# Sparse attention into a MoE layer on one core: rows loaded four to a partition, q/k transposes three tiles earlier, score tiles in front of the MoE units

## The chip, the cores and the metric

One core of a Trainium2 chip runs the kernel. The metric is device time in microseconds (us), lower is better; each median is of several executions on a chip. A "run" below also has one profiled execution, and its profile is what the lines are taken from. All medians are of fast runs alone: runs over 1.5% above the fastest of their kernel are left out. Engines: PE does matmuls, DVE is the vector engine, ACT the scalar engine, POOL is GpSimd, SP issues DMAs and does nothing else in this kernel. In this kernel matmuls write tiles in PSUM and the other tiles lie in SBUF; to "evict" is to copy a result from PSUM to SBUF. The "granted clock" is the share of PE's full clock that the profile records.

## The reference

Per head (8 batches x 8 heads, 576 rows, 64 columns):

```python
scores = scale * q @ k.T
thresh = max(scores, axis=-1) - tau
attn   = softmax(where(scores >= thresh, scores, -1e9))
x      = attn @ v                       # heads put side by side: [4608 tokens, 512]
h = x @ w_in                            # 512 -> 2048
out = leaky_relu(h, 0.01) @ w_out       # 2048 -> 512
```

## The kernel before

Two heads make a pair; a pair has five score tiles (four of 128 queries of both heads, a fifth "half" tile with the 64 last rows of each). A loop step handles two tiles; 160 tiles make 80 steps. MoE work is slipped into the steps: "h units" (first layer; 0.65 us of PE at full clock, 740.58 to 741.23 in the timeline), "o units" (second layer; 3.45 us, 743.36 to 746.81), and PV, the product of weights and v.

```python
def split(P):      # q, k -> high and low fp16 halves: ACT copy, POOL scale, POOL subtract
def turn_qk(P):    # one DMA transpose qk <- nat
def scores(P, i):  # score tile in PSUM, 128 x 1536 fp32, two buffers
def peak(s):       # DVE: mx = row maxima
def exps(s):       # ACT: bi = -mx, e = exp(S + bi)
def weights(s):    # DVE: th = mx - tau; w = (S >= th) * e with its sum; POOL: w *= 1 / sum
def pv(P):         # PE: p1 (512 queries), p2 (64); ACT evicts both into xT, later
# h units, o units and PV share one PSUM tag "m" with two buffers of 128 x 512 fp32

for n in range(0, NT + 10, 2):
    ...
    live.append(scores(tile n)); feed_h(2 or 3); live.append(scores(tile n + 1))
    feed_o()                                  # PV if one is due, else an o unit
    for s in live: peak(s); exps(s)
    for s in live: weights(s)
    flush(evacs)                              # eviction of PV or of the o unit
    for s in turned: turn_w(s)                # DMA transposes of the weights
    ...
    if i == 1: split(P + 2)
    if i == 3: turn_qk(P + 1)
    if i == 3 and P % 2 == 1: load(P + 3), load(P + 4)
```

The kernel issues everything through its class `InOrder`, which keeps the instructions in the order of the program.

## Time and profile before

| | before |
|---|---|
| median (3 runs) | 793.09 us |
| PE / DVE / ACT / POOL busy | 69 / 62 / 50 / 47% |
| mean granted PE clock | 0.836 |
| DVE idle before a row maximum, waiting for scores | 208.1 us |
| PE idle before score matmuls, waiting for the q/k transpose | 134.2 us |

No engine is full, so the waits matter. These lines are from the page's busy times and from the waits view (who waited <- for whom: us in all, times, longest):

```profile
PE 549.5 (69%) x3360; PEld 240.4 (30%) x3360; DVE 487.6 (62%) x1056; ACT 398.6 (50%) x773; POOL 370.0 (47%) x446
DVE mx L31 <- PE S L31: 208.1, 81, 25.2
PE S L31 <- DMA qk<-nat: 134.2, 21, 26.1
PE S L31 <- DVE w L31: 100.9, 48, 5.6
```

DVE waits for PE, and PE mostly for one DMA. Of the 134.2 us, 17.9 are the start of the program and 26.1 one wait while the MoE weights load; the other 19 waits sum to 90.2. In the timeline (start, duration, engine, operation; in brackets the idle time before and what ended it) one such wait looks so:

```profile
200.03 3.45 SPq L31 DMA_TRANSPOSE qk<-nat  x1
205.31 3.72 PE L31 MATMUL S<-qk 64*128 64x512 f16 x18 [6.65 <-DMA qk<-nat]
207.25 1.36 DVE L31 TENSOR_REDUCE mx<-S 128x2 f32<-128x1152 f32 x1 [4.71 <-PE S L31]
212.55 1.09 PE L31 MATMUL S<-qk 64*128 64x512 f16 x9
```

PE was ready at 198.66 (205.31 - 6.65), and the transpose was issued only at 200.03. After the wait, 18 score matmuls take 3.72 us, at a granted clock of 0.50; a few us later, nine take 1.09 at 1.00.

The threshold `th` is two numbers per partition and yet sometimes takes 2 us. The first line below is a tile view (min/median/max ns), the others are the timeline:

```profile
L31 DVE TENSOR_SCALAR th<-mx x160: 132/149/2548, 22.9 to 731.3; 128x2 f32<-128x2 f32 x128, 128x1 f32<-128x1 f32 x32
307.55 2.61 POOL L31 TENSOR_TENSOR nat<-sc,nat 128x1280 f16<-128x1280 f32 x1
308.16 2.03 DVE L31 TENSOR_SCALAR th<-mx 128x2 f32<-128x2 f32 x1
310.28 0.82 DVE L31 SCALAR_TENSOR_TENSOR w<-S,th,e 128x576 f16<-128x576 f32 x1
```

It ends when POOL's subtraction does (307.55 + 2.61 = 310.16). So do the others: each of the 32 thresholds of over 300 ns in this trace ends within 60 ns of the end of a POOL instruction of the split. That is what "blocked by POOL" means below.

### The profile page before, as it was taken

Reading aid. Unit: us, or ns where it says so; the run is one execution under the profiler, and the core shown is the slowest. Engines: PE = TensorE matmul, PEld = TensorE weight load, DVE = VectorE, ACT = ScalarE, POOL = GpSimd, SP = SyncE. Lnnn points to the kernel's source line nnn. Section 1 sums busy time; section 2 is a strip of 40 time slices with the busy share of each in tenths; the row PEclk is TensorE's granted clock in tenths of the full one; section 3 lists DMA queues with packets and bytes.
Section 4 is the critical chain, followed back from the end, with each engine's and each line's share of the span. In section 5 each row is a group of like instructions: output and inputs, shape, how many; then the busy total and the mean of one; then the engine's idle time right before and its main releaser. Section 6 shows DMA issues by size and latency. Waiting matters only on the chain. (4 is left out here: it accounts for less than half of the span.)

```text
span 791.8 us, 10563 instructions
## 1 busy us (share of the span) xinstructions
PE 549.5 (69%) x3360; PEld 240.4 (30%) x3360; DVE 487.6 (62%) x1056; ACT 398.6 (50%) x773; POOL 370.0 (47%) x446
## 2 busy tenths in 40 slices
PE   0440555768666769698775769698785769598998
PEld 0110121323222334234232334233232324243443
DVE  0870777757676667768675667768575667767000
ACT  1440444645454446657454546657454546656333
POOL 6570464454545454555445454555445544623000
PEclk9755675769888789889888789899887789989999
DMA  9689867694869867695769667695859677645201
GB/s 139 128 146 184 172 111 145 102 172 71 167 127 147 130 126 143 121 166 112 160 117 173 118 126 144 113 179 115 160 105 186 105 128 143 118 94 110 64 28 53
DMA packets 377624, 101.90 MB, mean 129 GB/s; under 512 B 370400, under 2 KB 372448, under 8 KB 377568
## 3 DMA queue, kind: packets, MB, share of 16 engines
q1 hardware_dynamic: 337984, 92.31, 61.7%
q0 software_dynamic: 39584, 8.91, 12.2%
q8 instruction: 26, 0.43, 0.2%
q14 instruction: 30, 0.25, 0.1%
HBM read 36.70 MB, written 9.44 MB: 58 GB/s over the span
## 5 line engine op out<-in xcount | busy, mean ns | idle before, releaser
L31 PE MATMUL S<-qk 64*128 64x512 f16 (+2 forms) x1344 | 216.6, 389 | 235.6 <-DMA qk<-nat 134.2
L31 POOL TENSOR_SCALAR w<-w,rc 128x576 f16<-128x576 f16 (+1 forms) x288 | 213.0, 751 | 351.2 <-issue 196.3
L31 DVE TENSOR_REDUCE mx<-S 128x2 f32<-128x1152 f32 (+1 forms) x160 | 198.1, 1242 | 208.6 <-PE S L31 208.1
L31 DVE SCALAR_TENSOR_TENSOR w<-S,th,e 128x576 f16<-128x576 f32 (+1 forms) x288 | 227.4, 823 | 19.6 <-ACT e L31 6.1
L31 ACT ACTIVATE e<-S,bi 128x576 f16<-128x576 f32 (+1 forms) x288 | 200.9, 743 | 5.2
L31 PEld LDWEIGHTS <-qk 64*128 64x128 f16 (+1 forms) x1344 | 74.0, 106 | 391.7 <-DMA qk<-nat 137.3
L31 ACT ACTIVATE gT<-hp 128x384 f16<-128x384 f32 x192 | 94.1, 490 | 186.6 <-PE hp L31 186.4
L31 PE MATMUL op<-w_out_85,gT 128*128 128x512 f16 x576 | 130.3, 380 | 0.0
L31 ACT ACTIVATE bi<-mx 128x2 f32<-128x2 f32 (+1 forms) x160 | 32.1, 201 | 145.6 <-DVE mx L31 145.5
L31 PEld LDWEIGHTS <-w_in_84 128*128 128x128 f16 x768 | 84.1, 112 | 68.6 <-issue 38.6
L31 POOL TENSOR_TENSOR nat<-sc,nat 128x1280 f16<-128x1280 f32 x32 | 83.5, 2609 | 3.9 <-ACT nat L31 1.3
L31 PE MATMUL hp<-xT_86,w_in_84 128*128 128x384 f16 x192 | 73.1, 381 | 2.8 <-ACT xT_88 L31 1.7
L31 PEld LDWEIGHTS <-gT 128*128 128x128 f16 x576 | 55.5, 98 | 61.5 <-issue 1.0
L31 PE MATMUL hp<-xT_87,w_in_84 128*128 128x384 f16 x192 | 72.9, 380 | 0.0
L31 PE MATMUL hp<-xT_88,w_in_84 128*128 128x384 f16 x192 | 72.6, 378 | 0.0
L31 PE MATMUL hp<-xT_89,w_in_84 128*128 128x384 f16 x192 | 71.5, 373 | 0.0
L31 DVE TENSOR_SCALAR th<-mx 128x2 f32<-128x2 f32 (+1 forms) x160 | 53.0, 331 | 0.0
L31 ACT ACTIVATE ob<-op 128x512 f32<-128x512 f32 x36 | 21.5, 597 | 38.1 <-PE op L31 38.1
L31 DVE RECIPROCAL rc<-su 128x2 f32<-128x2 f32 (+1 forms) x160 | 26.4, 165 | 16.9 <-DVE w L31 0.9
L31 PEld LDWEIGHTS <-vt 128*64 128x64 f16 x576 | 24.0, 119 | 21.1 <-issue 8.1
L31 DVE DVE_READ_ACCUMULATOR w<-S,th,e 128x1 f32 x288 | 23.9, 83 | 0.0
L31 ACT ACTIVATE nat<-raw_69 128x1280 f16<-128x1280 f32 x16 | 20.3, 1266 | 6.6 <-DMA raw_69<-in_k_dram 5.9
(186 smaller groups left out, 203.6 us busy)
## 6 DMA issues: line engine op xcount, KB each, us to landing
out_dram<-ob SPq DMA_DIRECT2D x36, 256.0 KB, 2.6
vt<-in_v_dram POOLq DMA_DIRECT2D x8, 576.0 KB, 10.8
raw_69<-in_q_dram SPq DMA_DIRECT2D x32, 128.0 KB, 3.6
raw_69<-in_k_dram SPq DMA_DIRECT2D x32, 128.0 KB, 5.9
raw_70<-in_q_dram SPq DMA_DIRECT2D x32, 128.0 KB, 2.7
raw_70<-in_k_dram SPq DMA_DIRECT2D x32, 128.0 KB, 2.7
W<-w SPq DMA_TRANSPOSE x128, 3.3
w_in_84<-in_moe_w_in_dram POOLq DMA_DIRECT2D x1, 2048.0 KB, 15.6
```

Of the source, the lines that this page charges most:

```text
L31: return self._tc.keep_in_program_order(f(*a, **k))
```

## The change

The intent: larger pieces in the loads, q/k ready in time, second score tile not behind the h units, a threshold that does not meet POOL. Four things change together.

```diff
@@ loads: partition p takes rows 4p .. 4p+3 of a head, 1 KB in one piece; tails of 64 rows apart
-  raws [128, 2, 2, 5, 128]; per pair 128-row blocks of 256 B pieces; vz tiles for the v tails
+  raws [128, 2, 4, 5, 64];  v in vts [128, 8, 5, 64]; no vz
+  main = src[...].rearrange("(h r) d -> h r d", h=n)[:, 0:512, :]
+  dma(out=dst[:, :, 0:4, :]..., in_=main.rearrange("h (p c) d -> p h (c d)", c=4))
@@ split: ACT and POOL copy q and k apart, permuting (h c d) to (c h d)
@@ weights
-  nc.vector.tensor_scalar(out=th, in0=mx, scalar1=-tau_f * UNIT, scalar2=None, op0=ALU.add)
+  nc.vector.scalar_tensor_tensor(out=th, in0=mx, scalar=-tau_f * UNIT, in1=mx, op0=ALU.add, op1=ALU.min)
@@ pv: tile i now holds queries 4t + i, so the eviction puts the tokens back in order
-  nc.scalar.activation(out=xT[g][:, b*S : b*S+512], in_=p1[:, :], func=AF.Copy, ...)
+  nc.scalar.activation(
+      out=xT[g][:, b*S : b*S+512].rearrange("p (t i) -> p i t", i=4),
+      in_=p1[:, :].rearrange("p (i t) -> p i t", i=4), func=AF.Copy, ...)
@@ loop (nh h units are due in a step; tile n's scores were issued at the end of the last step)
-  scores(n); feed_h(nh); scores(n + 1); feed_o(); peak, exps of both; weights of both; flush(evacs)
+  scores(n + 1); peak, exps of both; feed_o(); flush(evacs); feed_h(nh - 1)
+  weights of both; scores(n + 2); feed_h(1)
-  if i == 3: turn_qk(P + 1)
+  if i == 0: turn_qk(P + 1)
```

More of the change, by code (lines that the diff above doesn't have):

```diff
@@ L89 @@
     nc.gpsimd.memset(M2[32:33, 0:64], -60000.0)
-    raws = [sb.tile([128, 2, 2, 5, 128], FP32, name=f"raw_{i}") for i in range(2)]
-    vzs = [sb.tile([128, 2, 64], FP16, name=f"vz_{i}") for i in range(3)]
+    raws = [sb.tile([128, 2, 4, 5, 64], FP32, name=f"raw_{i}") for i in range(2)]
+    vts = [sb.tile([128, 8, 5, 64], FP16, name=f"vt_{i}") for i in range(2)]
     for t in raws:
-        nc.gpsimd.memset(t[0:64, :, :, 4, 64:128], 0.0)
-        nc.gpsimd.memset(t[64:128, :, :, 4, 0:64], 0.0)
-    for t in vzs:
-        nc.gpsimd.memset(t[64:128, 0, :], 0.0)
-        nc.gpsimd.memset(t[0:64, 1, :], 0.0)
+        for h in range(4):
+            nc.gpsimd.memset(t[64 - h % 2 * 64 : 128 - h % 2 * 64, :, h, 4, :], 0.0)
+    for t in vts:
+        for h in range(8):
+            nc.gpsimd.memset(t[64 - h % 2 * 64 : 128 - h % 2 * 64, h, 4, :], 0.0)
     w_in16 = sb.tile([128, NG, d_ff], FP16, name="w_in16")
@@ L104, with heads @@
     pairs = {}
-    vb = {}
+    def heads(dma, dst, src, r0, n):
+        part = src[r0 : r0 + n * S, :].rearrange("(h r) d -> r h d", h=n)
+        main = src[r0 : r0 + n * S, :].rearrange("(h r) d -> h r d", h=n)[:, 0:512, :]
+        dma(out=dst[:, :, 0:4, :].rearrange("p h c d -> p h (c d)"), in_=main.rearrange("h (p c) d -> p h (c d)", c=4))
+        for ab in range(2):
+            dma(out=dst[ab * 64 : ab * 64 + 64, ab::2, 4, :], in_=part[512:576, ab::2, :])
     def load(P):
@@ L110, in load @@
         raw = raws[P // 2 % 2]
+        vt = vts[P // 4 % 2]
         if P % 4 == 0:
-            vb[P // 4] = sb.tile([128, 36, 64], FP16, tag="vt", bufs=2, name="vt")
-            nc.gpsimd.dma_start(
-                out=vb[P // 4][:, :, :], in_=vf[r0 : r0 + 4608, :].rearrange("(c p) d -> p c d", p=128)
-            )
-        for t, (src, oB, tB) in enumerate(((qf, S, S + 512), (kf, S + 64, S))):
-            for ab, o in enumerate((0, oB)):
-                nc.sync.dma_start(
-                    out=raw[:, P % 2, t, 0:4, ab * 64 : ab * 64 + 64],
-                    in_=src[r0 + o : r0 + o + 512, :].rearrange("(c p) d -> p c d", p=128),
-                )
-            if P % 2 == 0:
-                two = src[r0 : r0 + 4 * S, :].rearrange("(u r) d -> r u d", u=2)
-                nc.sync.dma_start(out=raw[0:64, :, t, 4, 0:64], in_=two[512:576])
-                nc.sync.dma_start(out=raw[64:128, :, t, 4, 64:128], in_=two[tB : tB + 64])
-        pairs[P] = dict(raw=raw[:, P % 2], vt=vb[P // 4][:, P % 4 * 9 : P % 4 * 9 + 9, :])
+            heads(nc.gpsimd.dma_start, vt, vf, r0, 8)
+        if P % 2 == 0:
+            for t, src in enumerate((qf, kf)):
+                heads(nc.sync.dma_start, raw[:, t], src, r0, 4)
+        pairs[P] = dict(raw=raw[:, :, P % 2 * 2 : P % 2 * 2 + 2], vt=vt[:, P % 4 * 2 : P % 4 * 2 + 2])
     def split(P):
@@ L131, in split @@
         d["nat"] = nat
-        r2 = d["raw"].rearrange("p t s c -> p t (s c)")
-        sc = sb.tile([128, 2, 640], FP32, tag="sc", bufs=1, name="sc")
-        nc.scalar.activation(out=nat[:, 0, :, :], in_=r2, func=AF.Copy, bias=0.0, scale=PRE)
-        nc.gpsimd.tensor_scalar(out=sc[:, :, :], in0=r2, scalar1=PRE, scalar2=0.0, op0=ALU.mult, op1=ALU.add)
-        nc.gpsimd.tensor_tensor(out=nat[:, 1, :, :], in0=sc[:, :, :], in1=nat[:, 0, :, :], op=ALU.subtract)
+        sc = sb.tile([128, 2, 2, 5, 64], FP32, tag="sc", bufs=1, name="sc")
+        nc.gpsimd.tensor_scalar(
+            out=sc[:, :, :, :, :].rearrange("p t h c d -> p t (h c d)"),
+            in0=d["raw"].rearrange("p t h c d -> p t (h c d)"),
+            scalar1=PRE, scalar2=0.0, op0=ALU.mult, op1=ALU.add,
+        )
+        for t in range(2):
+            o = [nat[:, x, t, :].rearrange("p (c h d) -> p c h d", c=5, h=2) for x in range(2)]
+            nc.scalar.activation(
+                out=o[0], in_=d["raw"][:, t].rearrange("p h c d -> p c h d"), func=AF.Copy, bias=0.0, scale=PRE
+            )
+            nc.gpsimd.tensor_tensor(
+                out=o[1], in0=sc[:, t].rearrange("p h c d -> p c h d"), in1=o[0], op=ALU.subtract
+            )
     def turn_qk(P):
@@ L142, in turn_qk @@
         d["qk"] = qk[:, :, :].rearrange("p a b -> p (a b)")
-    def prep_v(P):
-        d = pairs[P]
-        vz = vzs[P % 3]
-        for ab in range(2):
-            h = slice(ab * 64, ab * 64 + 64)
-            nc.gpsimd.tensor_scalar(
-                out=vz[h, ab, :], in0=d["vt"][h, 4, :], scalar1=1.0, scalar2=0.0, op0=ALU.mult, op1=ALU.add,
-            )
-        d["vz"] = vz
     QH, KH, QL, KL = 0, 640, 1280, 1920
@@ L212, in weights @@
         th = sb.tile([128, 2], FP32, tag="th", bufs=4, name="th")
-        nc.vector.tensor_scalar(out=th[:, 0:n], in0=mx[:, 0:n], scalar1=-tau_f * UNIT, scalar2=None, op0=ALU.add)
+        nc.vector.scalar_tensor_tensor(
+            out=th[:, 0:n], in0=mx[:, 0:n], scalar=-tau_f * UNIT, in1=mx[:, 0:n], op0=ALU.add, op1=ALU.min
+        )
         for h, (po, eo, wd) in enumerate(spans):
@@ L242, in pv @@
         done[0] = P + 1
-        W, Wm, vt, vz = d["W"], d["Wm"], d["vt"], d["vz"]
+        W, Wm, vt = d["W"], d["Wm"], d["vt"]
         b, g = divmod(P, NG)
         p1 = ps.tile([128, 512], FP32, tag="m", bufs=2, name="p1")
-        for n in range(5):
-            for ab in range(2):
-                c = n + 5 * ab if n < 4 else 4
-                lhsT = vt[:, c, :] if n < 4 else vz[:, ab, :]
-                nc.tensor.matmul(
-                    out=p1[ab * 64 : ab * 64 + 64, 0:512], lhsT=lhsT, rhs=W[:, :, c, :],
-                    start=n == 0, stop=n == 4, skip_group_check=True,
-                )
         p2 = ps.tile([128, 512], FP32, tag="m", bufs=2, name="p2")
@@ L258, in pv @@
                 nc.tensor.matmul(
-                    out=p2[ab * 64 : ab * 64 + 64, 0:64], lhsT=vt[:, c, :], rhs=Wm[:, n, ab * 64 : ab * 64 + 64],
+                    out=p1[ab * 64 : ab * 64 + 64, :], lhsT=vt[:, ab, n, :], rhs=W[:, :, c, :],
+                    start=n == 0, stop=n == 4, skip_group_check=True,
+                )
+        for n in range(5):
+            for ab in range(2):
+                nc.tensor.matmul(
+                    out=p2[ab * 64 : ab * 64 + 64, 0:64], lhsT=vt[:, ab, n, :], rhs=Wm[:, n, ab * 64 : ab * 64 + 64],
                     start=n == 0, stop=n == 4, skip_group_check=True,
@@ L263, in evac @@
         def evac():
-            nc.scalar.activation(out=xT[g][:, b * S : b * S + 512], in_=p1[:, :], func=AF.Copy, bias=0.0, scale=1.0)
+            nc.scalar.activation(
+                out=xT[g][:, b * S : b * S + 512].rearrange("p (t i) -> p i t", i=4),
+                in_=p1[:, :].rearrange("p (i t) -> p i t", i=4), func=AF.Copy, bias=0.0, scale=1.0,
+            )
             nc.scalar.activation(
@@ L328 @@
     split(1)
-    prep_v(0)
     for P in range(2, 4):
@@ L334 @@
     hrate, hdebt = 2.8, 0.0
+    live = [scores(0, 0)]
     for n in range(0, NT + 10, 2):
-        two = [divmod(m, 5) for m in (n, n + 1) if m < NT]
         turned, stored = turns[:], stores[:]
         del turns[:], stores[:]
-        live = []
-        for x, (P, i) in enumerate(two):
-            live.append(scores(P, i))
-            if x == 0:
-                hdebt = min(hdebt + hrate, 4.0)
-                feed_h(int(hdebt))
-                hdebt -= int(hdebt)
-        if not two:
-            feed_h(4)
-        feed_o()
+        hdebt = min(hdebt + hrate, 4.0)
+        nh = int(hdebt) if n < NT else 4
+        hdebt -= nh
+        if n + 1 < NT:
+            live.append(scores(*divmod(n + 1, 5)))
         for s in live:
@@ L351 @@
             exps(s)
+        feed_o()
+        flush(evacs)
+        feed_h(nh - 1)
         for s in live:
@@ L354 @@
             turns.append(s)
-        flush(evacs)
+        live = [scores(*divmod(n + 2, 5))] if n + 2 < NT else []
+        feed_h(1)
         for s in turned:
@@ L358 @@
         flush(stored)
-        for P, i in two:
+        for m in (n, n + 1):
+            P, i = divmod(m, 5)
             if i == 1 and P + 2 < NP:
                 split(P + 2)
-            if i == 4 and P + 1 < NP:
-                prep_v(P + 1)
-            if i == 3 and P + 1 < NP:
+            if i == 0 and P + 1 < NP:
                 turn_qk(P + 1)
@@ L368 @@
                 load(P + 4)
+            P, i = divmod(m - 7, 5)
+            if i == 0 and 0 <= P < NP:
+                pq.append(P)
         if n == 4:
@@ L372 @@
             nc.gpsimd.dma_start(out=w_out16[:, :, :], in_=moe_w_out.rearrange("(j p) f -> p j f", p=128))
-        for m in (n, n + 1):
-            P, i = divmod(m - 7, 5)
-            if i == 0 and 0 <= P < NP:
-                pq.append(P)
         while given < NGRP and (given + 1) * GT <= (done[0] // NG) * S:
```

## The prediction

> **What bounds it now.** No engine is full: the page gives PE 69%, DVE 62%, ACT 50%, POOL 47% of 791.8 us. The scores-to-weights loop runs from 17.9 us (first score matmul) to about 732 us, 80 steps of two tiles, 8.9 us each; a 60 us tail is pure MoE matmuls at full clock. In the loop the DVE does 488 us of work and the waits view charges 208 us of its idling to score matmuls (mx <- PE S). Of that, 134 us in 21 waits is PE waiting for the q/k transpose (PE S <- DMA qk<-nat): 26 us once around 53-79 us, while the MoE weights load, then 3.4 to 7.7 us at most even pairs. After each such wait a score tile takes 1.90 us instead of 1.09 us. [...] The rest, some 70-90 us (about 1 us a step), is the second score tile standing behind three first-layer MoE units.
>
> **What the change does.**
> 1. q/k transposes three tiles earlier. Lead grows from under one step to more than one, against a 3.4 us issue and 5.2 us landing. I expect the 108 us of later waits to nearly vanish and the 26 us wait to halve: about -105 us of waiting, but the PE then meets the next limit, so about -90 us of span.
> 2. Row loads: 1 KB pieces instead of 256 B (v: 512 B written instead of 128 B). From 73.7k q/k and 36.9k v packets to about 25k and 12k. The queues now take 62% and 12% of the DMA engines' span. The 250k packets of the transposes stay. Worth mainly shorter landings; not on the chain except around 45-100 us. -5 us.
> 3. Score tiles first. R n+1 no longer waits for three MoE units, about -0.7 us per step; but in steps with a second-layer unit (3.5 us) or a PV product, the next first tile now waits for that unit, its eviction (queued behind the exponentials) and two MoE units. I compute about 6.8 us for empty steps, 7.4 for PV steps, 7.9 for second-layer steps; mean near 7.4 against 7.5 now (traced step without q/k wait). Net -10 us.
> 4. th: mean 331 ns because it sometimes takes up to 2.55 us, ending with a POOL nat subtraction; unblocked it is 0.15 us, so 29 us are blocked. [...] I expect the new form still to block, but on halved POOL pieces: -12 us.
> 5. Two half-size ACT copies for one: 1.27 to about 1.5 us, +7 us of ACT, hidden. vz copies vanish (15 us of POOL, hidden). Start about even.
>
> Sum: -117 from 793, less about 20 us given back, as POOL, ACT and second-layer steps become the limit. Predicted **695 us**, range 660 to 735. Faster by over 2%: 0.97; within 2%: 0.02; slower: 0.01.
>
> **What would show it.** PE S <- DMA qk waits under 30 us; mean clock 0.88 or more; th mean under 0.25 us; DMA packets near 304k; DVE busy near 470 us; step period near 7.5 us; tail still about 60 us; DVE idle before mx falling from 208 to about 120 us, charged to PE.
>
> **What would make it wrong.** Higher: permuted ACT/POOL patterns running slower than contiguous ones; ACT waiting for the bigger raw loads; eviction order blocking the two MoE accumulators; q/k transposes still queued behind weight transposes. Lower: th no longer blocking at all, and DVE saturating near 6.5 us a step (about 640 us).

Two passages are cut where marked: one on the PE clock, and the reason given in point 4 for the new threshold still being blocked. -90, -5, -10 and -12 us make the -117, and 20 given back lead to about 695. "After each such wait" is nearly so: of the 18 waits of over 1.5 us for the q/k transpose after the start, 17 were followed by a score tile's nine matmuls in 1.89 or 1.90 us at a granted clock of 0.50; after the one at 514.92 us they took 1.09 at 1.00.

## The result, and the profile after

The median is 738.87 us (three runs, 731.19 to 741.89). A ratio is the mean time of one kernel's fast runs over that of the other's in the same rounds, so it is not quite the ratio of the medians: 0.930 (95% interval 0.919 to 0.942). It is faster, but above the range. A later control with five runs gave 737.74 us and 0.928 (0.925 to 0.931), so the miss is no scatter.

The same views of the changed kernel:

```profile
PE 524.4 (72%) x3360; PEld 229.8 (31%) x3360; DVE 485.1 (67%) x1056; ACT 420.5 (58%) x805; POOL 365.4 (50%) x444
DVE mx L31 <- PE S L31: 112.4, 105, 20.4
PE S L31 <- DVE w L31: 111.0, 57, 17.7
PE hp L31 <- ACT xT_99 L31: 21.8, 7, 3.2
PE hp L31 <- ACT xT_100 L31: 20.7, 7, 3.1
PE S L31 <- DMA qk<-nat: 18.5, 1, 18.5
PE hp L31 <- ACT xT_101 L31: 16.1, 6, 3.2
PE hp L31 <- ACT xT_102 L31: 8.8, 3, 2.9
```

The transpose waits are gone: the one left is the start of the program (18.5 us, 17.9 before). But ACT has 22 us more to do, and a new wait of 67 us (the four xT lines added) stands where before had none worth showing (2.2 us): h units wait for the eviction of PV. One step with a PV, from the timeline:

```profile
320.88 1.27 PE L31 MATMUL p_3191<-W,vt_72 128*64 128x512 f16 x10
320.99 1.36 DVE L31 TENSOR_REDUCE mx<-S 128x2 f32<-128x1152 f32 x1 [0.85 <-PE S L31]
322.62 1.37 ACT L31 ACTIVATE e<-S,bi 128x576 f16<-128x576 f32 x2
323.88 1.31 ACT L31 ACTIVATE xT_100<-p_3191 128x512 f16<-128x512 f32 x1
325.24 0.32 PE L31 MATMUL hp<-xT_99,w_in_97 128*128 128x384 f16 x1 [2.93 <-ACT xT_100 L31]
326.63 1.09 PE L31 MATMUL S<-qk 64*128 64x512 f16 x9
327.76 1.36 DVE L31 TENSOR_REDUCE mx<-S 128x2 f32<-128x1152 f32 x1 [1.91 <-PE S L31]
```

PV fills both "m" buffers and is done at about 322.3. Its eviction comes behind the exponentials of both tiles and then takes 1.31 us; in the kernel before, the same 128x512 eviction took 0.60:

```profile
228.62 0.60 ACT L31 ACTIVATE xT_89<-p_1813 128x512 f16<-128x512 f32 x1
```

PE stands for 2.93 us, the next score tile is late, DVE idles 1.91.

Steps fall into five classes, since two pairs are five steps: A (tiles 0 and 1), B (2, 3), C (4 and the next pair's 0), D (1, 2), E (3, 4). C and E hold the PV products. Mean us from one step's first row maximum to the next one's, from the 14th step on, as I took them from the timeline:

| kernel | A | B | C | D | E |
|---|---|---|---|---|---|
| before | 9.20 | 8.86 | 7.97 | 7.41 | 10.85 |
| changed | 7.76 | 7.66 | 8.44 | 7.40 | 8.54 |

The prediction gave 7.9 us to steps with an o unit (A and B, often D: measured 7.4 to 7.8, about right), and 7.4 to those with PV (C and E: measured 8.4 and 8.5). This profile is of the fastest of the three runs; the control's profile (740 us) has C at 8.99 and the others within 0.2 us.

Early, while the MoE weights load, the stall stays. Timeline:

```profile
43.84 0.83 POOL L31 DMA_DIRECT2D w_in_97<-in_moe_w_in_dram  x1
43.92 19.25 SPq L31 DMA_TRANSPOSE W<-w  x3
59.38 1.19 POOL L31 DMA_DIRECT2D w_out_98<-in_moe_w_out_dram  x1
68.04 6.16 SPq L31 DMA_DIRECT2D raw_69<-in_k_dram  x3
86.63 0.74 ACT L31 ACTIVATE nat<-raw_69 128x640 f16<-128x640 f32 x1 [4.89 <-DMA raw_69<-in_k_dram]
88.90 0.82 DVE L31 SCALAR_TENSOR_TENSOR w<-S,th,e 128x576 f16<-128x576 f32 x1 [14.61 <-ACT e L31]
```

The row of three transposes spans 19.25 us: their issues took 1.29, 10.28 and 3.80 us of SP's queue (median of all W transposes 1.30), with 3.8 us between the first two, and they landed 19.2, 20.2 and 15.3 us after issue (median 3.3). The row loads issued behind them landed 13.4 to 18.0 us after issue (medians of the whole run 4.7 for q and 5.1 for k), ACT waits for rows in front of its exponentials, and DVE idles 14.61 us. I read it as the same stall with another name: before, PE waited 26.1 us for qk.

The threshold, in the tile view:

```profile
L31 DVE SCALAR_TENSOR_TENSOR th<-mx x160: 139/150/1382, 23.5 to 664.2; 128x2 f32<-128x2 f32 x128, 128x1 f32<-128x1 f32 x32
```

The longest fell from 2548 to 1382 ns, the length of a halved POOL subtraction (1398 ns), but the mean only from 331 to 301. Again all 36 thresholds of over 300 ns end within 60 ns of the end of a POOL instruction of the split.

### The profile page after: what moved, and what is told of

Read it like the earlier page. It is cut to its first block, busy times and chain, and to the rows that moved or that the text cites. A ratio compares the mean times of both kernels' runs of the same rounds, so it can differ in the third digit from the quotient of the medians.

```text
span 729.4 us, 10446 instructions
## 1 busy us (share of the span) xinstructions
PE 524.4 (72%) x3360; PEld 229.8 (31%) x3360; DVE 485.1 (67%) x1056; ACT 420.5 (58%) x805; POOL 365.4 (50%) x444
## 2 busy tenths in 40 slices
DMA packets 302614, 101.88 MB, mean 140 GB/s; under 512 B 270816, under 2 KB 297440, under 8 KB 302560
## 5 line engine op out<-in xcount | busy, mean ns | idle before, releaser
L31 PE MATMUL S<-qk 64*128 64x512 f16 (+2 forms) x1344 | 205.7, 374 | 130.2 <-DVE w L31 111.0
L31 PEld LDWEIGHTS <-qk 64*128 64x128 f16 (+1 forms) x1344 | 72.2, 103 | 285.2 <-issue 125.7
L31 PE MATMUL op<-w_out_98,gT 128*128 128x512 f16 x576 | 132.8, 385 | 1.2 <-ACT xT_102 L31 1.2
L31 PE MATMUL hp<-xT_99,w_in_97 128*128 128x384 f16 x192 | 66.6, 347 | 69.2 <-ACT xT_99 L31 21.8
L31 PEld LDWEIGHTS <-w_in_97 128*128 128x128 f16 x768 | 76.0, 103 | 122.4 <-issue 86.0
L31 POOL TENSOR_TENSOR nat<-sc,nat 128x640 f16<-128x640 f32 x64 | 88.1, 1398 | 3.0 <-POOL sc L31 0.4
L31 PE MATMUL hp<-xT_102,w_in_97 128*128 128x384 f16 x192 | 67.9, 354 | 0.0
L31 PE MATMUL hp<-xT_101,w_in_97 128*128 128x384 f16 x192 | 67.8, 353 | 0.0
L31 PE MATMUL hp<-xT_100,w_in_97 128*128 128x384 f16 x192 | 67.3, 350 | 0.0
L31 DVE SCALAR_TENSOR_TENSOR th<-mx 128x2 f32<-128x2 f32 (+1 forms) x160 | 48.2, 301 | 0.0
L31 ACT ACTIVATE nat<-raw_69 128x640 f16<-128x640 f32 x32 | 21.8, 730 | 25.2 <-issue 20.3
L31 POOL TENSOR_SCALAR sc<-raw_69 128x1280 f32<-128x1280 f32 x16 | 20.2, 1263 | 14.3 <-DMA raw_69<-in_k_dram 14.1
```

Source lines behind the costliest of these rows:

```text
L31: return self._tc.keep_in_program_order(f(*a, **k))
```

## The experiments

All were correct against the reference. Each was timed in five rounds (4 to 6 runs) beside the kernel before, whose median stayed at 792 to 794 us. The runs of a letter share a chip and the letters do not, so comparisons such as d1 against c5 or c1 against the changed kernel cross chips; the kernel before differed by under 0.2% between them.

| run | median us | ratio to before (95%) |
|---|---|---|
| changed, again | 737.74 | 0.928 (0.925 to 0.931) |
| c1 plain eviction | 711.62 | 0.897 (0.894 to 0.900) |
| c3 old threshold | 734.79 | 0.927 (0.925 to 0.929) |
| c4 old order | 725.53 | 0.916 (0.914 to 0.917) |
| c5 before + early transposes | 710.75 | 0.897 (0.893 to 0.901) |
| d1 old order + plain eviction | 699.62 | 0.884 (0.880 to 0.887) |
| d2 c1 + early eviction | 682.09 | 0.861 (0.858 to 0.864) |
| e2 changed + early eviction | 697.86 | 0.881 (0.878 to 0.883) |
| e3 d2 with the old loads | 687.21 | 0.867 (0.864 to 0.871) |
| d3 d2 + weights in pieces | 666.62 | 0.843 (0.839 to 0.847) |
| d4 d2 + maxima in PSUM | 675.46 | 0.852 (0.849 to 0.855) |
| e1 d2 + both (d3's pieces moved) | 663.78 | 0.837 (0.834 to 0.840) |

### c1: the eviction written contiguously

```diff
-  out=xT[...].rearrange("p (t i) -> p i t", i=4), in_=p1[:, :].rearrange("p (i t) -> p i t", i=4)
+  out=xT[...], in_=p1[:, :]
@@ o unit's store: columns are out of order, so rows go out with a stride of four
-  nc.sync.dma_start(out=out[r : r + 128, :], in_=ob[:, :])
+  rows = out[b*S : b*S+512, :].rearrange("(t i) d -> t i d", i=4)   # per half, or whole where it can be
+  nc.sync.dma_start(out=rows[c % 128 : c % 128 + n, c // 128, :], in_=ob[p0 : p0 + n, :])
```

> The changed kernel with the PV eviction written contiguously again (no 4-element stride); the token order is put right in the output store instead, whose rows go out with a stride of four rows. Same result. Theory 1 (the strided eviction is what makes PV steps long): the large eviction goes from 1.30 to about 0.60 us, PV steps (classes C and E) from about 8.5 to about 7.8 us, PE hp <- ACT xT waits from 67 to about 45 us, time about 20 us below the changed kernel (about 718 where that is 738). Rival (PV steps are long only because the eviction stands behind two tiles of exponentials; its length does not matter): the eviction gets shorter, but the time moves by under 6 us.

711.62 us, 26 below the changed kernel; theory 1's size was about right, its rival (under 6 us) falls. The new stores cost nothing that shows: they landed in a median of 2.5 to 2.7 us, against 2.4. The tile and waits views:

```profile
L31 ACT ACTIVATE xT<-p x64: 218/411/598, 53.2 to 656.6; 128x512 f16<-128x512 f32 x32, 128x64 f16<-128x64 f32 x32
PE hp L31 <- ACT xT L31: 51.9, 23, 2.5
```

The eviction is 598 ns at most. The wait shrank from 67 to 52 us and is still large, so the place of the eviction costs as well; that is d2's question.

### c3: the old threshold

```diff
-  nc.vector.scalar_tensor_tensor(out=th, in0=mx, scalar=-tau_f * UNIT, in1=mx, op0=ALU.add, op1=ALU.min)
+  nc.vector.tensor_scalar(out=th, in0=mx, scalar1=-tau_f * UNIT, scalar2=None, op0=ALU.add)
```

> The changed kernel with the threshold as tensor_scalar again. If the new two-input form is blocked by POOL as the old one was, th means are both about 0.30 to 0.33 us and the time is within 5 us of the changed kernel. If the new form is the better one by what the prediction gave it (12 us), this run is 8 to 16 us slower.

734.79 us: the intervals overlap, no difference shown. Groups by shape say why: with the old form the two-column thresholds average 321 ns and the one-column ones 139; with the new form 302 and 298. The new form only lets the one-column thresholds be blocked too; the 139 ns says that in the old form they were not. Why the form matters to them was not shown.

### c4: the old order in a step

```diff
-  scores(n + 1); peak, exps; feed_o(); flush(evacs); feed_h(nh - 1); weights; scores(n + 2); feed_h(1)
+  scores(n); feed_h(nh); scores(n + 1); feed_o(); peak, exps; weights; flush(evacs)
```

> The changed kernel with the old order in a step (first tile, MoE units, second tile, second-layer unit; eviction after the weights), early transposes kept. My prediction gave the new order 10 us: then this run is about 748. Rival: with the long eviction and the two accumulators the new order costs as much as it gives, and this run is equal to the changed kernel or faster (under 738). Steps of class D (no second-layer unit or PV) should lengthen from 7.4 to 7.5, C and E shorten by up to 1 us.

725.53 us. The new order, to which the prediction gave a gain of 10, costs 12. The rival was right. By class, in the manner of the table above, this run has A 8.15, B 8.52, C 7.37, D 8.09, E 7.55: the new order gains in A, B and D and loses about 1 us in each PV step. The expectation was wrong that D holds no o unit: 9 of its 14 steps in the table do.

### c5: the kernel before, with early transposes alone

```diff
-            if i == 3 and P + 1 < NP:
+            if i == 0 and P + 1 < NP:
                 turn_qk(P + 1)
```

> The kernel before with nothing changed but the q/k transpose issued at the first tile of a pair rather than the fourth. If the 108 us of later q/k waits are worth what the prediction took (about 90 us together with half of the early one), this run alone is at about 705 to 715; if the waits turn into other waits, it stays above 730. The early stall at 53 to 79 us: halved if lead matters, about 25 us still if the weight loads block the queue whatever the lead.

710.75 us, as the expectation for "the waits are worth their time" had it: one changed digit gains 82 us and beats the whole change by 27. What is left of the wait is mostly the start of the program (18.1 us):

```profile
PE S L31 <- DMA qk<-nat: 22.6, 3, 18.1
```

The early stall did not halve: its longest step is 22.8 us (31.4 in the kernel before; the changed one has two, 14.9 and 21.7).

### d1: old order and plain eviction together

> The changed kernel with both the old order in a step and the contiguous eviction (output rows put right by the store). It is the kernel before with early transposes (710.8 us) plus the row loads, split copies and new threshold. If the row loads are worth anything in the steady loop, it is 5 to 10 us below that run, 701 to 706; if they are off the path, it is within 4 us of it. Against the old order with the strided eviction (725.5) it tells what the strided eviction costs in the old order: about 15 to 20 us if its length is on the path there too.

699.62 us. Four kernels now make a square, and its effects add: the strided eviction costs 26 us in the new order (737.7 against 711.6) and 26 in the old one (725.5 against 699.6); the new order costs 12 with either eviction. Where it costs shows without the stride too: from d1 to c1 the steps with PV go from 7.35 to 8.14 (C) and 7.17 to 7.83 us (E), the others from 7.71 to 7.58 (A), 8.20 to 7.69 (B) and 7.27 to 7.53 (D). Against c5, what is left of the change (row loads, split copies, no vz, threshold; and d1's strided stores) gains 11 us, a little more than the first expectation; that the stride would cost only 15 to 20 us in the old order was too low. In the old order h units hardly wait for the eviction (PE hp <- ACT xT: 2.2 us in d1, against 51.9 in c1), since the next score tile stands between PV and the next h unit.

### d2: evict PV between the two tiles' exponentials

```diff
+  pv_step = bool(pq)
   for x, s in enumerate(live):
       peak(s); exps(s)
+      if pv_step and x == 0:
+          feed_o(); flush(evacs)
-  feed_o(); flush(evacs)
+  if not pv_step or not live:
+      feed_o(); flush(evacs)
```

> The contiguous-eviction run, and in PV steps the product is issued and evicted between the two tiles' exponentials instead of behind both. Theory (PV steps are long since the MoE units wait for both accumulators to be evicted, and the eviction waits for two tiles of exponentials): PE hp <- ACT xT waits fall from 52 to under 15 us, classes C and E from 8.1 and 7.8 to about 6.7, A, B and D stay; about 675 to 690 us. Rival (another wait, on DVE or the score buffers, is right behind): waits move elsewhere and the time stays above 704.

682.09 us, 30 below c1. C and E went to 6.99 and 6.93 us (c1: 8.14 and 7.83). One PV step in the timeline:

```profile
310.47 1.27 PE L31 MATMUL p<-W,vt 128*64 128x512 f16 x10
311.78 0.71 ACT L31 ACTIVATE xT<-p 128x512 f16<-128x512 f32 x2 [0.82 <-PE p L31]
312.43 1.46 PE L31 MATMUL hp<-xT,w_in 128*128 128x384 f16 x8 [0.53 <-ACT xT L31]
312.62 1.37 ACT L31 ACTIVATE e<-S,bi 128x576 f16<-128x576 f32 x2
313.82 1.09 PE L31 MATMUL S<-qk 64*128 64x512 f16 x9
```

PE waits 0.53 us where the changed kernel waited 2.93 and c1 up to 2.5. The sum of these waits is 23.5 us, not below the 15 that was expected, but the time is in the stated range. With this in place the new order beats the old one (682 against 700). The old order with an early eviction was not run; since its h units wait only 2.2 us for the eviction (d1), little is to be expected of it, but that is argued and not shown.

### e2: the strided eviction, evicted early

> The changed kernel (strided eviction kept) with only the PV product and its eviction moved between the two tiles' exponentials: the fourth cell of length against place. If length and place act separately, the strided eviction costs 23 to 27 us here too (about 706). If the early place gives the eviction room, most of its 0.7 us is hidden and the run is within 10 us of the contiguous early one (682): then the place is the cause and the length only a size.

697.86 us, 16 above d2: between the two expectations. The early place hides 10 of the 26 us that the stride costs. Length and place are two causes, and they overlap in part: moving the eviction gains 40 us with the long one and 30 with the short one.

### e3: the best order with the old loads

The loop of d2 in the kernel before, whose tokens need no reordering; loads, split, vz and threshold as before.

> The kernel before with early transposes, the new order in a step and the early eviction, but the old row loads, copies, vz and threshold (so contiguous eviction and store by nature). Against the early-eviction run (682) it gives the worth of the row loads where the loop is tightest. If the loads matter as the old-order pair showed (11 us), it is at about 690 to 695; if that was the threshold or the batch, within 4 us of 682.

687.21 us, with an interval (0.8635 to 0.8713) that barely overlaps d2's (0.8583 to 0.8640). By the medians the row loads and what comes with them are worth 5 us here, not quite clear of noise, and 11 in the old order. Which of the parts earns it was not separated.

### d3: weights in pieces

```diff
-  n == 4: w_in whole; n == 8: w_out whole
+  n in (2, 6, 10, 14): a quarter of w_in; n in (18, 22, 26, 30): a quarter of w_out
```

> The early-eviction run, with each MoE weight matrix loaded in four pieces four tiles apart, w_in from tile 2, w_out from tile 18, instead of two whole loads at tiles 4 and 8. If the stall at 58 to 88 us is a burst (weights, raw rows and v at once, in front of transposes), the two long steps (13.4 and 21.7 us) fall to about 8 each and the run gains 15 to 22 us on the early-eviction run. If the DMA engines are short over the whole first 110 us, the stall is spread over more steps and the gain is under 6 us.

666.62 us, 15 below d2, at the lower end of the gain expected of a burst; the fast runs spread from 665 to 673. The first 13 steps took 98.7 us instead of 113.4 and none over 10.6, but one later step of 18.5 us appeared: a q/k transpose was late by 9.2 us, which I put down to a piece of w_out meeting a v load. The stall was mostly a burst; part of it moved. The landings say the same: with the 2 MB of w_in issued by POOL in one piece, SP's slowest weight transposes landed 20.2 us after issue in the changed kernel and 17.4 in d2, against a median of 3.3; in d3's first 130 us the slowest took 12.6. A piece of w_in landed in 6.2 us in d3, the whole in 17.3 in d2.

### d4: row maxima in PSUM

```diff
-  mx = s["mx"] = sb.tile([128, 2], FP32, tag="mx", bufs=4, name="mx")
+  mx = s["mx"] = pt[:, 700:702]        # columns of the score tile that nothing uses
```

and the threshold again a tensor_scalar, now with a PSUM input.

> The early-eviction run, with the row maxima kept in unused columns of the score tile in PSUM, so that the threshold instruction reads no SBUF tensor. If blocking by POOL's SBUF access is what stretches the threshold (mean 0.32 us), its mean falls to 0.2 us or below with a maximum under 0.4 us. If that blocked time is on the path, the run is 10 to 20 us below the early-eviction run; if it is hidden, within 4 us.

```profile
L31 DVE TENSOR_SCALAR th<-S x160: 136/150/161, 23.4 to 614.7; 128x2 f32<-128x2 f32 x128, 128x1 f32<-128x1 f32 x32
```

No threshold is over 161 ns any more, where the same instruction reading SBUF took up to 1403 ns in c3: moving the source out of SBUF ends the blocking. The gain is 6.6 us (intervals apart), between the two expectations: of 23 us of blocking in the profile (d2's mean against 150 ns) less than a third was on the path. Even that is an upper bound: the same edit lets ACT's `bi` read the maxima from PSUM, which took its median from 203 to 172 ns, 5 us over 160 tiles, in front of the exponentials. The two were not separated.

### e1: all together

d4, with the pieces at tiles 2, 4, 10, 12 and 14, 18, 22, 24, away from row and v loads.

> Contiguous eviction, early eviction, maxima in PSUM, and the weights in eight pieces placed between the row and v loads. If the gains of the threshold (6.6 us) and of the spread weights (12 us) add, and the 9 us transpose wait left by the first spread goes, 655 to 664 us; if they share a wait, no less than 668.

663.78 us, at the end of the first range: it is 18 below d2, where the two gains, 6.6 and 15, would make 22, so most of it adds. The 9.2 us wait went, but one of 5.9 us for a q/k transpose is left at 74.5 us. This is the best version, 10% below the changed kernel.

```profile
PE 507.5 (77%) x3360; PEld 227.7 (35%) x3360; DVE 465.4 (71%) x1056; ACT 390.1 (59%) x805; POOL 367.5 (56%) x450
```

### f1: the changed kernel again

> The changed kernel again, as the reference for the other runs: its first three runs spread from 731 to 742 us. If 738.9 was typical, the median is 736 to 741 and old-form threshold (734.8) and this agree within 5 us; if the first runs were scattered by chance, the median falls to about 733 and the differences from the contiguous eviction (711.6) and the old order (725.5) shrink to about 21 and 8 us.

737.74 us (734.73 to 740.23); the first three runs were typical.

## Why the prediction was wrong

The direction and the main cause were right, the sum was not: 98 us expected, 54 measured (55 in the control). The path from before to after, by medians: 793.1, early transposes alone 710.8 (-82), loads, split and threshold 699.6 (-11), strided eviction 725.5 (+26), new order 737.7 (+12).

1. **Early transposes, "about -90 us of span": -82, nearly right.** The later waits vanished as said, but they were 90 us and not 108: the prediction counted the start's 17.9 us among them, which stays. "The 26 us wait to halve" failed: the step that holds the stall went from 31.4 to 22.8 us (c5). Spreading the weight loads left no step over 10.6 us in that stretch (d3).
2. **Row loads, "-5 us", and threshold, "-12 us": -11 together.** That they come near each other is luck: the threshold was worth nothing that shows (c3), the rest about 11. That the new form still blocks was right (301 ns mean), but it gains nothing over the old one (c3), and the predicted mean of "under 0.25 us" was wrong. Packets came out as predicted (302,614 against 304k).
3. **"Score tiles first ... Net -10 us": +12.** This step failed. Its term "7.4 for PV steps" measured 8.4 and 8.5, and 8.1 and 7.8 without the stride (c1): PE waits for the eviction of both accumulators, and with the eviction moved forward the same steps take 7.0 and 6.9 (d2). I saw that the eviction is queued behind the exponentials and that PV takes both accumulators, named it as a risk, and still gave the step 7.4 us.
4. **The strided eviction is in no term of the sum: +26.** The diff changes one line's access pattern; I costed the split copies, which are permuted as well (1.27 us predicted to become 1.5, measured 2 x 0.73), and not the eviction, which went from 0.60 to 1.30 us (128x512 fp16 written at a step of four elements, PSUM read contiguously as before). "Permuted ACT/POOL patterns running slower" was listed among the risks without a size.
5. **"About 20 us given back."** Its mechanism, "POOL, ACT and second-layer steps become the limit", was not worked out and is not what came: it was the PV steps that became long, and no engine is full (ACT 58%, POOL 50%). Errors 3 and 4 (22 and 26 us), with 8 and 6 us missing from 1 and 2, make 62; the 20 us set aside leave 42 of them, and the miss is 44 (43 in the control).

Of the signs that it named, the waits for the transpose (18.5 us, the start), the packets, the mean clock (0.873 to 0.888), the tail (64 us) and DVE's idle time before mx (112 us) came about as said. The threshold's mean, DVE's busy time (485 us, not 470) and the step period (about 8.0 us in the table, not 7.5) did not.

The low case, "th no longer blocking at all", is nearly empty: removing all blocking gave at most 6.6 us, in d2's loop (d4).

A wait can go with a lower clock too. In c1's timeline, after 2.22 us of waiting for the eviction, nine score matmuls took 1.89 us instead of 1.09; in the kernel before, nine took 1.90 at a granted clock of 0.50 and 1.09 at 1.00:

```profile
239.61 1.72 PE L31 MATMUL hp<-xT,w_in 128*128 128x384 f16 x8 [2.22 <-ACT xT L31]
241.27 1.89 PE L31 MATMUL S<-qk 64*128 64x512 f16 x9
```

In the profiles of the kernel before and of the changed one the granted clock is full or half, in stretches of 3.41 us or multiples of it. From 100 us after the start to 80 before the end, 54 full-clock stretches of 3.41 us were followed by half clock, and PE was busy under 0.46 of each; 194 were followed by full clock, and PE was busy over 0.40 of each (over 0.45 in all but three). So PE was not always idle throughout before the clock fell, and in these two traces a busy share of about 0.45 divides the cases; no run was made to test it. How much of the 26 us is clock and how much is wait was not separated.

## What to carry to other kernels

When a layout change must be undone somewhere, look for a place that nothing waits for: here strided rows of an output DMA, not a strided write on an engine that PE waits for. When an instruction order is turned round, follow each shared buffer to the instruction that frees it, and look at what stands before that one on its own engine. Test the parts of a change alone: one digit of this one was worth more than the whole.
